# Dilated window attention with low-rank experts: batch rows as units, block-diagonal v, eight shared PSUM banks and an own list schedule

## The chip, the cores and the metric

The kernel runs on one core of one Trainium2 chip. The metric is device time in microseconds (us); lower is better. Kernel and changed kernel were each run twice for the main comparison. The kernel before took 156.75 us (median; 155.86 to 157.65). Each execution also leaves a span, from its first to its last instruction, which is 1.7 to 2.1 us shorter than its time in all runs of the record (1.8 in the profiled run of the changed kernel). A run counts as slow when it is over 1.5% above the fastest of its kernel.

Engine names in the profile: PE is the matmul engine (PEld its weight loads), DVE the vector engine, ACT the scalar engine, POOL the general engine that also issues the casting loads, SP the queue that issues stores. PSUM is the memory that matmuls write to; both kernels divide it into banks of 512 float32 columns, eight in all.

## The reference, cut to what matters

Eight batch rows, eight heads, 576 tokens, head dimension 64, float32. Heads 0 to 3 look back over 32 tokens, heads 4 to 7 over every fourth of 128. Then every token goes through two of eight rank-16 adapters.

```python
scores = scale * np.matmul(q, k.transpose(0, 1, 3, 2))
mask_plain = (rel >= 0) & (rel < 32)
mask_dil = (rel >= 0) & (rel < 128) & (rel % 4 == 0)
attn = softmax(np.where(mask, scores, -1e9))      # plain for heads 0-3, dilated for 4-7
x = np.matmul(attn, v)                            # then (B*S, H*D) = (4608, 512)
logits = x @ w_gate                               # 8 experts, the top two, weights by softmax
out = x + sum(w[e] * (x @ A[e]) @ B[e] for e in top2)
```

Names used below: the gates are `x @ w_gate` and all `x @ A` in one block of matmuls; the routing picks the top two experts; gz is `x @ A` times the chosen weights; the deltas are gz `@ B`, added to x at the end. aw holds A and w_gate, bt holds B.

Both kernels sort the tokens of the dilated heads by their remainder modulo 4, so that these heads become banded too. Keys come in blocks of 64 and each block is scored against the 96 queries that can see it. Inputs lie in memory as float32 and are cast to bf16 by the loads.

## The kernel before: the parts that matter here

All 4608 tokens are one stream, cut into nine units of 512 tokens; heads are taken in pairs (hp), one head on partitions 0 to 63, the other on 64 to 127. Per pair: a mask matmul for each of two banks, score matmuls on top, one exponential, value matmuls, normalisation by the sum column of v.

```python
ps_s = tile_pool(name="ps_s", bufs=2, space=PSUM)   # scores: 2 buffers of two banks
ps_o = tile_pool(name="ps_o", bufs=1, space=PSUM)   # values: one buffer of two banks
ps_m = tile_pool(name="ps_m", bufs=2, space=PSUM)   # transposes, gates, deltas
...
load(0); load(1)
nc.gpsimd.dma_start(out=AW, in_=aw)
nc.gpsimd.dma_start(out=BT, in_=bt)
nc.vector.tensor_scalar(BT, in0=BT, scalar1=0.5, scalar2=None, op0=ALU.mult)
...
def values(t, hp):                 # pairs of 64-row matmuls, one bank for each head of the pair
    ...
    for a in range(2):
        rows = slice(64 * a, 64 * a + 64)
        nc.tensor.matmul(op[:, a, 65 * u : 65 * u + 65],
                         lhsT=p[rows, at : at + 128], rhs=V[tv][rows, hp, blk], ...)
...
def after(t, hp):                  # gates and deltas of unit t-1, while unit t attends
    ...
steps = [(t, hp) for t in range(NU) for hp in range(4)]
for n, (t, hp) in enumerate(steps):
    scores(*steps[n + 1]); values(t, hp); after(t, hp)   # (cut)
```

The order on each engine is made from this program by a scheduler. Each unit's result is stored from a rotating buffer as soon as it is done.

The softmax here doesn't subtract the row's maximum and nothing guards it: scores larger than these inputs give would overflow.

Of the kernel before, what the change touches and what calls it, by code (L numbers as in the profile page):

```python
# [10 lines left out]
FP = mybir.dt.float32  # L11
# [5 lines left out]
NEG = -30000.0  # L17
B, H, S, D = 8, 8, 576, 64
W, C = 32, 4
E, R = 8, 16  # L20
NT = B * S
NU = NT // 512
ER = E * R
SEG = 96
PER = 192


def band(edges):


    k = np.arange(64)[:, None]
    w = np.arange(96)[None, :]
    ok = (w >= k) & (w - k < W)
    for e in edges:
        ok &= ~((k < e) & (w >= e))
    return np.where(ok, 0.0, NEG).astype(np.float32)


def masks():


    reg, cut = band(()), band((64,))
    mp = np.concatenate([reg, reg, cut, reg, reg, reg], 1)
    md = []
    for t in range(NU):
        edges = [144 * b for b in range(1, B)]
        first = band([e - 128 * t for e in edges])
        second = band([e - 128 * t - 64 for e in edges])
        before = band([e - 128 * t + 64 for e in edges])
        md += [first, second[:, 0:64], before[:, 64:96]]  # L50
    m = np.concatenate([mp] + md, 1)
    return np.concatenate([m, m], 0).astype(ml_dtypes.bfloat16)


NM = 6 * SEG + NU * 2 * SEG
# [3 lines left out]
def attn_adapters_kernel(  # L59
    ctx: ExitStack,  # L60
    tc: tile.TileContext,
    kq: bass.AP,
    vin: bass.AP,
    aw: bass.AP,
    bt: bass.AP,
    mk: bass.AP,
    idn: bass.AP,
    outp: bass.AP,
    outd: bass.AP,
):  # L70



# [4 lines left out]
    xpool = ctx.enter_context(tc.tile_pool(name="x", bufs=3))  # L78
    mpool = ctx.enter_context(tc.tile_pool(name="m", bufs=2))
    ps_s = ctx.enter_context(tc.tile_pool(name="ps_s", bufs=2, space=bass.MemoryType.PSUM))  # L80
    ps_o = ctx.enter_context(tc.tile_pool(name="ps_o", bufs=1, space=bass.MemoryType.PSUM))
    ps_m = ctx.enter_context(tc.tile_pool(name="ps_m", bufs=2, space=bass.MemoryType.PSUM))

    KQ = [one.tile([128, 4, 2, 512], BF, name=f"kq{t}") for t in range(NU)]
    V = [one.tile([128, 4, 8, D + 1], BF, name=f"v{t}") for t in range(NU)]
    ident = one.tile([128, 128], BF, name="ident")
    MK = one.tile([128, NM], BF, name="mk")
    AW = one.tile([128, 4, ER + E], BF, name="aw")
    BT = one.tile([ER, H * D], BF, name="bt")
    NP = 4  # L90
    P = [one.tile([128, 8 * PER], BF, name=f"p{i}") for i in range(NP)]

    nc.sync.dma_start(out=ident, in_=idn)
    nc.sync.dma_start(out=MK, in_=mk)
    for i in range(NP):
        nc.vector.memset(P[i].rearrange("p (s c) -> p s c", c=PER)[:, :, SEG:PER], 0.0)

    def load(t):
        if t == 0:
            for hp in range(4):  # L100
                nc.gpsimd.dma_start(out=KQ[t][:, hp], in_=kq[t, :, hp])
                nc.gpsimd.dma_start(out=V[t][:, hp], in_=vin[t, :, hp])
        else:
            nc.gpsimd.dma_start(out=KQ[t], in_=kq[t])
            nc.gpsimd.dma_start(out=V[t], in_=vin[t])

    load(0)
    load(1)
    nc.gpsimd.dma_start(out=AW, in_=aw)
    nc.gpsimd.dma_start(out=BT, in_=bt)  # L110
    nc.vector.tensor_scalar(BT, in0=BT, scalar1=0.5, scalar2=None, op0=ALU.mult)
    for t in range(2, NU):
        load(t)

    def prob(t, hp):
        return P[(4 * t + hp) % NP]

    def scores(t, hp):
        sp = ps_s.tile([128, 2, 512], FP, name="sps")
        for bk in range(2):  # L120
            if hp < 2:
                at = 0
                reg = True
                if t % 2 and t < 8 and (t - 1) // 4 == bk:
                    at = 2 if (t - 1) % 4 == 0 else 0
                    reg = False
                if reg:
                    mask = MK[:, 3 * SEG : 4 * SEG].unsqueeze(1).to_broadcast([128, 4, SEG])
                else:
                    mask = MK[:, at * SEG : (at + 4) * SEG].rearrange("p (s c) -> p s c", c=SEG)  # L130
            else:
                m0 = 6 * SEG + t * 2 * SEG
                mask = MK[:, m0 : m0 + 2 * SEG].unsqueeze(1).to_broadcast([128, 2, 2 * SEG])
            nc.tensor.matmul(  # L134
                sp[:, bk, 0 : 4 * SEG], lhsT=ident, rhs=mask, start=True, stop=False, skip_group_check=True
            )
        todo = []
        for s in range(8):
            if hp < 2 and s < 7 or hp >= 2 and s % 2 == 0:
                todo.append((s, 0, t, s, s, SEG))  # L140
            else:
                todo.append((s, 0, t, s, s, 64))
                if t:
                    todo.append((s, 64, t - 1, s, 0 if hp < 2 else s - 1, 32))
        for s, col, tk, kb, qb, n in todo:
            for a in range(2):
                rows = slice(64 * a, 64 * a + 64)
                at = SEG * (s % 4) + col
                nc.tensor.matmul(  # L149
                    sp[rows, s // 4, at : at + n],  # L150
                    lhsT=KQ[tk][rows, hp, 0, 64 * kb : 64 * kb + 64],
                    rhs=KQ[t][rows, hp, 1, 64 * qb : 64 * qb + n],
                    start=False, stop=True, skip_group_check=True,
                )
        nc.scalar.activation(  # L155
            prob(t, hp).rearrange("p (b s c) -> p b s c", b=2, c=PER)[:, :, :, 0:SEG],
            sp[:, :, 0 : 4 * SEG].rearrange("p b (s c) -> p b s c", c=SEG),
            AF.Exp, scale=scale,
        )

    X = {}

    def values(t, hp):
        st, hh = divmod(hp, 2)
        if hh == 0:
            X[t, st] = xpool.tile([128, 4, 4, D], FP, name=f"x{st}")
        x = X[t, st]
        p = prob(t, hp)
        op = ps_o.tile([128, 2, 512], FP, name="ops")
        for u in range(4):  # L170
            jobs = [(2 * u * PER, t, 2 * u), ((2 * u + 1) * PER - 64, t, 2 * u + 1)]
            if st == 0 and u:
                if (8 * t + 2 * u) % 9:
                    jobs.append(((2 * u - 1) * PER + 64, t, 2 * u - 1))
            elif st == 0:
                if t and (8 * t) % 9:
                    jobs.append((7 * PER + 64, t - 1, 7))
            elif t:
                jobs.append(((2 * u + 1) * PER + 64, t - 1, 2 * u + 1))
            for n, (at, tv, blk) in enumerate(jobs):  # L180
                for a in range(2):
                    rows = slice(64 * a, 64 * a + 64)
                    nc.tensor.matmul(  # L183
                        op[:, a, 65 * u : 65 * u + 65],
                        lhsT=p[rows, at : at + 128], rhs=V[tv][rows, hp, blk],
                        start=(n == 0), stop=(n == len(jobs) - 1), skip_group_check=True,
                    )
        o = op[:, :, 0 : 4 * 65].rearrange("p a (u d) -> p a u d", u=4)
        rec = mpool.tile([128, 2, 4], FP, name="rec")
        nc.vector.reciprocal(rec, o[:, :, :, D])  # L190
        nc.vector.tensor_tensor(  # L191
            x[:, :, 2 * hh : 2 * hh + 2].rearrange("p u a d -> p a u d"),
            o[:, :, :, 0:D], rec.unsqueeze(3).to_broadcast([128, 2, 4, D]), ALU.mult,
        )
        xb = mpool.tile([128, 4, 2 * D], BF, name=f"xb{hp}")
        nc.gpsimd.tensor_copy(xb, x[:, :, 2 * hh : 2 * hh + 2].rearrange("p u a d -> p u (a d)"))
        X[t, "b", hp] = xb

    M = {}

    def turn(t, st):
        tp = ps_m.tile([128, 1024], BF, name="mps")
        tv = tp.rearrange("p (k u i) -> p k u i", k=2, u=4)
        for hh in range(2):
            for u in range(4):
                nc.tensor.transpose(tv[:, hh, u], X[t, "b", 2 * st + hh][:, u], ident)  # L206
        xt = mpool.tile([128, 2, 512], BF, name=f"xt{st}")
        nc.scalar.copy(xt, tp.rearrange("p (k n) -> p k n", k=2))
        M[t, "xt", st] = xt

    def gates(t):
        xtp = M[t, "xt", 0].rearrange("p k (i c) -> p k i c", c=C)
        xtd = M[t, "xt", 1].rearrange("p k (c i) -> p k c i", c=C)
        zs = mpool.tile([128, C, ER + E], FP, name="zs")
        for half in range(2):
            zp = ps_m.tile([128, 2, ER + E], FP, name="mps")
            for cc in range(2):
# [151 lines left out]
```

## Time and profile before

| | kernel before |
|---|---|
| time, median of 2 | 156.75 us |
| span of the profiled run | 152.2 us |
| first score matmul, last value matmul | 8.0 us, 132.2 us |
| PE busy | 107.8 us, 71% of the span |
| loads done | about 81 us |
| one unit from 82 to 134 us | 10.4 us |

From the profile's page: the span, the busy time of each engine, then the span in 40 slices (tenths busy of PE, the granted PE clock in tenths, the busy share of the DMA engines).

```profile
span 152.2 us, 4604 instructions
PE 107.8 (71%) x2036; PEld 73.8 (49%) x2036; DVE 74.3 (49%) x194; ACT 61.1 (40%) x91; POOL 36.6 (24%) x66
PE   0279165989689627869967979989979887467150
PEclk9999955699689995555899999999999999975555
DMA  3999999999999999999970600602405106006015
```

PE has holes in the first half, exactly while DMA is full, and its clock falls there. The windows view gives busy time by stage (start and end, length, then PE, PEld, DVE, ACT and POOL busy with instruction counts, granted clock, DMA share, GB/s):

```profile
8.00:132.00 124.00, 98.76 (x1984) 68.58 (x1986) 63.66 (x170) 56.64 (x84) 31.05 (x53) 0.88 0.71 174
12.00:50.00 38.00, 28.53 (x656) 18.79 (x655) 11.10 (x26) 12.15 (x15) 9.99 (x19) 0.82 1.06 215
50.00:81.00 31.00, 22.13 (x302) 15.23 (x300) 15.97 (x44) 13.98 (x22) 7.18 (x13) 0.72 0.98 233
81.00:132.00 51.00, 44.90 (x976) 32.40 (x977) 36.50 (x100) 28.89 (x45) 11.75 (x18) 1.00 0.26 106
```

The Trainium skill, "TensorE: Matmul & The Clock Gate", Part 1, says that PE runs at half rate by default and that sustained activity releases it. The trace agrees: where PE has holes, between 12 and 81 us, the mean granted clock is 0.72 to 0.82, and it is 1.00 once the work is dense. A hole on PE is thus paid twice. The clock row is not to be trusted at the very start: it shows full clock before 15 us, yet the same two mask matmuls took longer there than later in the timeline (start, duration):

```profile
11.79 0.82 PE L134 MATMUL sps<-mk,ident 128*128 128x384 bf16 x2
29.79 0.50 PE L134 MATMUL sps<-mk,ident 128*128 128x384 bf16 x2
```

What one unit costs on PE at the full clock can be read from the chain of waits (start, duration, work):

```profile
29.33 0.53 PE sps L149 x24
29.86 0.43 PE sps L134 x2
30.29 0.48 PE ops L183 x24
30.77 0.46 PE sps L149 x18
92.37 0.61 PE mps L278 x4
95.11 0.55 PE mps L206 x8
97.18 0.95 PE mps L221 x14
111.95 0.40 PE mps L261 x4
```

Per pair: masks 0.43, scores 0.46 or 0.53, values 0.48; per unit besides: transposes 2 x 0.55, gates 16/14 of 0.95, gz transposes 0.40, deltas 2 x 0.61.

Two lines of the waits view (who waited for whom: total us, times, longest): its largest wait, and the one for bt:

```profile
DVE rec L190 <- PE ops L183: 28.9, 18, 9.4
DVE bt L111 <- DMA bt<-in_bt_dram: 8.6, 1, 8.6
```

### The profile page before, as it was taken

The page shows a single profiled execution, that of the slowest core. Times are in us where ns is not written, and L with a number is a line of the kernel's source. Part 1 is how long each engine was busy: PE and PEld are TensorE (multiplying, and loading weights), DVE is VectorE, ACT ScalarE, POOL GpSimd, SP SyncE. Part 2 cuts the span into 40 slices and gives each one's busy share as a digit, 9 for nine tenths or more (in the row PEclk, how much of TensorE's full clock was granted, in tenths as well). Part 3 has the DMA queues.
Part 4 walks back from the last instruction along what each step waited for, and adds up shares of the span by engine and source line. Part 5 has one row for each costly group of instructions (what it writes and reads, how often), then busy time and mean ns, then how long its engine had stood idle before and what let it go on. Part 6 is the DMA issues. An engine that isn't in the chain of part 4 may idle for free.

```text
span 152.2 us, 4604 instructions
## 1 busy us (share of the span) xinstructions
PE 107.8 (71%) x2036; PEld 73.8 (49%) x2036; DVE 74.3 (49%) x194; ACT 61.1 (40%) x91; POOL 36.6 (24%) x66
## 2 busy tenths in 40 slices
PE   0279165989689627869967979989979887467150
PEld 0045033656356514746655756756847656335020
DVE  3003103344240066175568578387677777770560
ACT  3023212345134640452463565583764653413110
POOL 7445014111116920111102122111341221310000
PEclk9999955699689995555899999999999999975555
DMA  3999999999999999999970600602405106006015
GB/s 101 179 203 221 210 211 216 223 205 220 211 221 214 216 207 224 232 274 269 216 276 14 273 6 22 261 4 118 161 0 236 48 0 249 33 18 258 3 57 219
DMA packets 6644, 24.86 MB, mean 163 GB/s; under 512 B 864, under 2 KB 1632, under 8 KB 5600
## 3 DMA queue, kind: packets, MB, share of 16 engines
q0 software_dynamic: 3744, 14.50, 47.9%
q1 hardware_dynamic: 2880, 10.06, 16.8%
q8 instruction: 16, 0.26, 0.7%
q14 instruction: 4, 0.03, 0.1%
HBM read 29.62 MB, written 9.44 MB: 257 GB/s over the span
## 4 chain that ended last, share of the span: by engine, by line
PE 46%; DVE 21%; DMA 14%; ACT 10%; issue 5%; POOL 1%; ACTq 0%; DVEq 0%; POOLq 0%
PE sps L149 10%; DMA bt<-in_bt_dram 9%; PE sps L134 8%; PE ops L183 8%; PE mps L278 7%; PE mps L221 6%; DMA kq_73<-in_kq_dram 5%; PE mps L206 4%; DVE gz L250 4%; PE mps L261 3%; ACT zs L225 2%; ACT gt L263 2%; ACT p_96 L155 2%; DVE eq L231 1%; DVE ms L233 1%
## 5 line engine op out<-in xcount | busy, mean ns | idle before, releaser
L134 PE MATMUL sps<-mk,ident 128*128 128x384 bf16 x72 | 22.9, 385 | 9.0 <-DMA mk<-in_mk_dram 5.6
L190 DVE RECIPROCAL rec<-ops 128x8 f32<-128x8 f32 x36 | 7.3, 204 | 29.1 <-PE ops L183 28.9
L278 PE MATMUL mps<-bt,gt 128*128 128x256 bf16 x72 | 15.4, 326 | 4.1 <-ACT gt L263 2.1
L155 ACT ACTIVATE p_95<-sps 128x768 bf16<-128x768 f32 x9 | 7.3, 812 | 18.4 <-PE sps L149 16.3
L155 ACT ACTIVATE p_97<-sps 128x768 bf16<-128x768 f32 x9 | 7.3, 810 | 10.2 <-PE sps L149 8.4
L278 PEld LDWEIGHTS <-gt 128*128 128x128 bf16 x72 | 7.1, 115 | 8.5 <-issue 3.5
L155 ACT ACTIVATE p_96<-sps 128x768 bf16<-128x768 f32 x9 | 7.3, 811 | 9.2 <-PE sps L149 7.0
L155 ACT ACTIVATE p_98<-sps 128x768 bf16<-128x768 f32 x9 | 7.3, 812 | 7.9 <-PE sps L149 4.9
L261 PE MATMUL mps<-ident,gz 128*128 128x128 bf16 x36 | 4.1, 247 | 8.5 <-DVE gz L250 8.5
L225 ACT COPY zs<-mps 128x272 f32<-128x272 f32 x18 | 6.7, 387 | 7.7 <-PE mps L221 7.4
L134 PEld LDWEIGHTS <-ident 128*128 128x128 bf16 x72 | 5.3, 101 | 9.3 <-issue 4.8
L263 ACT COPY gt<-mps 128x512 bf16<-128x512 bf16 x9 | 5.3, 585 | 10.1 <-PE mps L261 10.1
L183 PEld LDWEIGHTS <-p_98 64*128 64x128 bf16 x208 | 4.3, 100 | 6.3 <-DVE x_269 L191 2.0
L261 PEld LDWEIGHTS <-gz 128*128 128x128 bf16 x36 | 2.4, 107 | 9.8 <-DVE gz L250 9.7
L149 PEld LDWEIGHTS <-kq_74 64*64 64x64 bf16 x84 | 3.8, 134 | 6.7 <-DMA kq_74<-in_kq_dram 5.0
L183 PEld LDWEIGHTS <-p_96 64*128 64x128 bf16 x208 | 4.7, 103 | 4.7 <-issue 3.8
L149 PE MATMUL sps<-kq_74 64*64 64x96 bf16 (+1 forms) x64 | 3.4, 253 | 4.6 <-DMA kq_74<-in_kq_dram 4.6
L149 PEld LDWEIGHTS <-kq_73 64*64 64x64 bf16 x84 | 4.0, 153 | 4.5 <-DMA kq_73<-in_kq_dram 4.4
L183 PEld LDWEIGHTS <-p_97 64*128 64x128 bf16 x208 | 4.5, 103 | 3.4 <-DVE tt L239 1.7
L183 PEld LDWEIGHTS <-p_95 64*128 64x128 bf16 x208 | 4.6, 101 | 2.2 <-issue 1.3
L149 PE MATMUL sps<-kq_73 64*64 64x96 bf16 (+1 forms) x64 | 3.1, 268 | 2.4 <-DMA kq_73<-in_kq_dram 2.4
L149 PEld LDWEIGHTS <-kq_75 64*64 64x64 bf16 x84 | 3.2, 108 | 2.6 <-issue 2.4
(359 smaller groups left out, 279.3 us busy)
## 6 DMA issues: line engine op xcount, KB each, us to landing
kq_73<-in_kq_dram POOLq DMA_DIRECT2D x4, 256.0 KB, 8.3
kq_74<-in_kq_dram POOLq DMA_DIRECT2D x1, 1024.0 KB, 12.3
kq_75<-in_kq_dram POOLq DMA_DIRECT2D x1, 1024.0 KB, 16.8
kq_76<-in_kq_dram POOLq DMA_DIRECT2D x1, 1024.0 KB, 22.3
kq_77<-in_kq_dram POOLq DMA_DIRECT2D x1, 1024.0 KB, 23.3
kq_78<-in_kq_dram POOLq DMA_DIRECT2D x1, 1024.0 KB, 27.5
kq_79<-in_kq_dram POOLq DMA_DIRECT2D x1, 1024.0 KB, 29.3
kq_80<-in_kq_dram POOLq DMA_DIRECT2D x1, 1024.0 KB, 30.1
```

The costliest lines, as they stand in the source:

```text
L134: nc.tensor.matmul(sp[:, bk, 0 : 4 * SEG], lhsT=ident, rhs=mask, start=True, stop=False, skip_group_check=True)
L149: nc.tensor.matmul(sp[rows, s // 4, at : at + n], lhsT=KQ[tk][rows, hp, 0, 64 * kb : 64 * kb + 64], rhs=KQ[t][rows, hp, 1, 64 * qb : 64 * ...
L155: nc.scalar.activation(prob(t, hp).rearrange("p (b s c) -> p b s c", b=2, c=PER)[:, :, :, 0:SEG], sp[:, :, 0 : 4 * SEG].rearrange("p b (s ...
L183: nc.tensor.matmul(op[:, a, 65 * u : 65 * u + 65], lhsT=p[rows, at : at + 128], rhs=V[tv][rows, hp, blk], start=(n == 0), stop=(n == len(j ...
L190: nc.vector.reciprocal(rec, o[:, :, :, D])
L206: nc.tensor.transpose(tv[:, hh, u], X[t, "b", 2 * st + hh][:, u], ident)
L221: nc.tensor.matmul(zp[:, cc], lhsT=xt, rhs=AW[:, kk], start=(kk == 0), stop=(kk == 3), skip_group_check=True,)
L225: nc.scalar.copy(zs[:, 2 * half : 2 * half + 2], zp)
L250: nc.vector.tensor_tensor(gz.rearrange("p c (e r) -> p c e r", e=E), zs[:, :, 0:ER].rearrange("p c (e r) -> p c e r", e=E), g2.unsqueeze(3 ...
L261: nc.tensor.transpose(tp[:, 128 * c : 128 * (c + 1)], M[t, "gz"][:, c], ident)
L263: nc.scalar.copy(gt.rearrange("p (i c) -> p i c", c=C), tp.rearrange("p (c i) -> p i c", c=C))
L278: nc.tensor.matmul(dp[:, a], lhsT=lhs, rhs=BT[:, 256 * st : 256 * st + 256], start=True, stop=True, skip_group_check=True,)
```

## The change

Its intent is to keep every engine filled. A unit becomes one whole batch row (576 tokens), so no band crosses a unit's edge. v is stored block-diagonally, the two heads of a pair on different partitions and columns with zeros between, so one 128-row matmul of 130 columns serves both heads and its result fits one bank. Rows live in a ring of four slots. PSUM becomes eight single banks that everybody shares. The output stays resident, and its stores wait for the last loads. The order on every engine comes from a list schedule in the kernel, with a duration for each operation.

```diff
-NT = B * S
-NU = NT // 512
+NB = 9
+NS = 4
+NP = 4
+class Op:  # name, engine, duration (ns), what it waits for, priority, banks it takes and frees
+class Plan:
+    def order(self):     # simulates the engines; the earliest start, then priority, wins
+        ...
+    BS = [psum.tile([128, 512], FP, name=f"bs{i}") for i in range(8)]
+    plan = Plan({"s": 8, "p": NP, "xb": 4, "xt": 2, "zs": 2, "gz": 2, "g": 2})
...
-        sp = ps_s.tile([128, 2, 512], FP, name="sps")
+            banks = [buf(("S", b, hp), BS, k) for k in range(2)]
+            for k in range(2):
+                rows = slice(64 * k, 64 * k + 64)        # masks: 64 rows each, side by side
...
-                for a in range(2):
-                    rows = slice(64 * a, 64 * a + 64)
-                    nc.tensor.matmul(
-                        op[:, a, 65 * u : 65 * u + 65],
-                        lhsT=p[rows, at : at + 128], rhs=V[tv][rows, hp, blk],
+                    nc.tensor.matmul(
+                        o[:, 130 * r : 130 * r + 130].rearrange("p (a d) -> p a d", a=2),
+                        lhsT=p[:, at : at + 128], rhs=bdv(b, hp, j),
...
+            nc.gpsimd.tensor_copy(                       # a new reorder of the gated tokens, on POOL
+                buf(("g", b), GN).rearrange("p (i c) -> p c i", c=C),
+                buf(("g", b), GD).rearrange("p (c i) -> p c i", c=C),
+            )
...
+    gate = f"L{B - 1}01"                                 # stores wait for the last row's first load
+        add(f"S{b}{hp}", "PE", 620, ...)                 # scores of a pair: planned 620 ns
+        add(f"V{b}{st}{k}", "PE", (440, 440, 530)[k], ...)
+        add(f"K{b}", "PE", 300, ...)                     # gz transposes
+        add(f"M{b}", "POOL", 680, ...)                   # the reorder
+    with tc.manual_schedule():
+        for op in plan.order():
+            op.emit()
```

gz moves from DVE to POOL, and the adapters' weights are loaded first on the SP queue and cast on ACT.

## The prediction

> **What bounds the kernel now.** Three stages, from the windows view. (a) 0 to about 25 us: little runs. PE waits 5.0 us for the second unit's keys, and DVE sits 8.6 us (waits view) in front of the scaling of bt, whose load queues behind 1.5 units of loads; the normalisations are behind it. DMA is saturated: 212 GB/s of bf16 written, so 424 GB/s of fp32 read. The Trainium skill, "DMA: Bandwidth & Descriptors", Specifications, gives 435 GB/s as the fabric ceiling; the trace agrees. (b) 25 to 134 us: PE-bound with gaps. From 82 to 134 us one unit of 512 tokens takes 10.4 us (start to start of the gate transposes in the chain of waits); PE is busy 44.6 of 52 us, DVE 38.0, ACT 28.7, DMA a quarter. Earlier the granted clock falls to 0.55 in places. (c) 134 to 152 us: the last unit's chain, PE clock 0.53.
>
> **What changes.** Eight units of 576 tokens instead of nine of 512 with seams.
> - PE: 2036 matmuls become about 1500. Values 832 -> 416: 130 columns on 128 rows instead of pairs of 65 columns on 64 rows; instructions fall, columns streamed don't. Masks: two 64-row matmuls (480, 384 columns) side by side instead of two of 384 in sequence. Per batch I estimate: scores with masks 2.6 us (18 score matmuls took 0.46 in the trace), values 52 x 57 ns = 2.9, transposes 1.1, gates 20 x 65 ns = 1.3, deltas 1.1: about 9.1 us.
> - DVE: normalisation in six pieces of 384 columns. From the trace (512 columns 692 ns, 8 columns 204 ns) a piece is about 560 + 200 ns; routing about 1.5 us, five additions 3.2 us: 9.3 us a batch. gz (0.69 us) moves to POOL, where it is slower.
> - ACT: exponentials 572 + 492 ns four times, transposed copies 2.9 us, the rest 1.8: 8.9 us a batch.
> - POOL: casts (0.61 us for 512 columns), gz, one reorder, load issues: about 7 us.
> - DMA: the same bytes in; 28.5 MB at 424 GB/s is 8.4 us a batch, ending near 72 us instead of 80. Stores (9.44 MB at about 390 GB/s, 24 us) wait until the last loads, then drain under compute.
>
> So all are balanced near 9 us a batch, and the gain is overlap: eight shared banks and ordering by list remove the waits for the single "ops" buffer and for whole stages, and bt no longer blocks DVE.
>
> **Sum.** First normalisation at about 11 us; eight batches at 9.3 us with about 93% filling = 80 us; the last batch's chain after its attention (cast, transpose, gates, routing, gz, transpose, delta, store), serial, about 11 us net of what is counted: span about 103 us. Unprofiled time is 4.5 us above the span before: **108 us, range 99 to 120**. Chances: faster by over 2% 0.97, within 2% 0.01, slower 0.02.
>
> **What would show it.** Loads ended by 70 to 76 us; no DVE wait over 3 us after the start; between 20 and 80 us PE, DVE and ACT each over 80% busy and a period of 9.5 to 10.5 us a batch; granted clock near 1 there; stores landing after 72 us, off the chain except the last; a serial tail of 12 to 18 us.
>
> **What would make it wrong.** A fixed order jams where real durations differ from the planned (POOL waiting for old loads in front of casts, gz above 1.5 us on POOL): period 11 to 12 us and 120 us or more. Half-width loads (64 partitions) running at less than full rate: loads bind at over 10 us a batch. Clock throttling under denser PE work.

## The result, and the profile after

The changed kernel took 121.39 us (median; 120.8 and 121.98). The ratio, that is the mean time of its fast runs over that of the kernel before in the same rounds (so not quite the ratio of the two medians), is 0.774, with a 95% interval of 0.760 to 0.788. The direction was right. The time lies 13.4 us above the stated 108 and outside the range of 99 to 120.

The page's lines of after:

```profile
span 119.0 us, 3669 instructions
PE 92.2 (77%) x1496; PEld 69.2 (58%) x1496; DVE 75.2 (63%) x220; ACT 70.4 (59%) x155; POOL 59.4 (50%) x86
PE   0105979999999999999999989999999915910540
PEclk9999999999999999999999999999999997695555
DMA  3999999999999999999999999998640053009054
```

The windows view of after:

```profile
9.00:95.00 86.00, 82.81 (x1429) 63.49 (x1430) 58.74 (x172) 59.94 (x137) 48.66 (x69) 1.00 0.93 227
95.00:119.00 24.00, 8.84 (x68) 5.56 (x67) 9.73 (x30) 4.48 (x11) 6.16 (x5) 0.67 0.36 147
20.00:91.00 71.00, 69.81 (x1234) 53.36 (x1233) 51.65 (x156) 50.32 (x117) 41.24 (x58) 1.00 0.96 241
```

From 20 to 91 us PE is busy 69.8 of 71 us at the full clock. In the waits view PE waits only 1.0 us in all from 20 to 95 us (four waits). DVE, whose 9.3 us a batch the prediction took for the period, is busy 51.7 of 71 us, ACT 50.3; so its sign "PE, DVE and ACT each over 80% busy" failed for both (73% and 71%). (The Trainium skill's front page, "Trainium Kernel Development and Optimization", Performance Expectations, warns that matmul busy time is a bad measure of closeness to the roofline, since matmuls are pipelined. It still named the right engine here, but only e1 below proves that.)

Where the 33 us of span went, divided at the start of the first score matmul and at the end of the last value matmul:

| stage | before | after |
|---|---|---|
| start to first score | 8.0 us | 9.4 us |
| first score to last value | 124.2 us | 85.9 us |
| last value to the end | 20.0 us | 23.7 us |

All of the gain is in the middle; the tail became longer, and the start differs by no more than it varies from run to run (see the experiments). What one row costs on PE now, from the chain of waits of after:

```profile
38.38 0.47 PE bs L329 x8
43.56 0.46 PE bs L462 x5
45.27 0.44 PE bs L486 x4
47.37 0.54 PE bs L486 x4
47.91 0.23 PE bs L498 x4
48.14 1.41 PE bs L403 x20
49.55 0.33 PE bs L371 x4
51.39 0.27 PE bs L290
51.66 0.52 PE bs L298 x18
52.18 0.39 PE bs L371 x5
61.52 0.81 PE bs L329 x14
62.33 0.24 PE bs L340 x4
```

Masks and scores 4 x 0.80 (0.27 and 0.53), values 2 x (0.47 + 0.81 + 0.24), transposes 2 x (0.33 + 0.39), gates 1.41, gz transposes 0.46, deltas 0.44 + 0.54 + 0.23: 10.8 us per 576 tokens. The gate blocks of successive rows start at 25.28, 36.64, 48.14, 59.37, 71.50, 82.77 and 91.80 us, 11.1 us apart on average (the first five intervals 11.5, the last 9.0). So the change took no work off PE (10.6 before, 10.8 after, for the same tokens): values became dearer, 3.0 us against 2.2, and masks with scores cheaper, 3.2 against 4.2. What it did was to fill PE and, with that, to hold its clock: 98.8 of 124 us busy at 0.88 became 82.8 of 86 us at 1.00. Of the 38 us, some 16 are thus shorter busy time, and 22 are idle time filled.

The tail, from the timeline of after (start, duration, engine, line, operation, and in brackets the idle time before it):

```profile
100.59 2.58 PE L403 MATMUL bs<-aw,xt 128*128 128x136 bf16 x20
103.70 2.48 DVE L508 TENSOR_TENSOR x<-x,bs 128x512 f32<-128x512 f32 x4 [5.87 <-PE bs L486]
106.43 0.19 DVE L424 TENSOR_REDUCE sm<-zs 128x5 f32<-128x40 f32 x1
108.54 1.27 POOL L449 TENSOR_TENSOR gz<-zs,sm 128x640 bf16<-128x640 f32 x1 [5.60 <-DVE sm L444]
111.45 1.46 POOL L472 COPY gn<-gd 128x576 bf16<-128x576 bf16 x1 [1.64 <-ACT gd L467]
114.82 0.41 DVE L515 TENSOR_TENSOR x<-x,bs 128x256 f32<-128x256 f32 x1
```

The last gates take 2.58 us instead of 1.4, because PE has gone cold. Their copies are done at 103.66 us, but the last routing starts at 106.43, since DVE first does row 6's additions. Then come gz, the reorder and the last additions, one after another.

### The profile page after: what moved, and what is told of

Its sections match the earlier page's. It is cut to its first block, busy times and chain, and to the rows that moved or that the text cites. A ratio compares the mean times of both kernels' runs of the same rounds, so it can differ in the third digit from the quotient of the medians.

```text
span 119.0 us, 3669 instructions
## 1 busy us (share of the span) xinstructions
PE 92.2 (77%) x1496; PEld 69.2 (58%) x1496; DVE 75.2 (63%) x220; ACT 70.4 (59%) x155; POOL 59.4 (50%) x86
## 4 chain that ended last, share of the span: by engine, by line
PE 60%; DMA 13%; DVE 8%; POOL 8%; issue 5%; POOLq 1%; ACT 1%; DVEq 0%; ACTq 0%
PE bs L329 14%; DMA slot<-in_kv_dram 13%; PE bs L298 12%; PE bs L403 10%; PE bs L371 6%; PE bs L290 6%; PE bs L486 5%; DVE x L508 3%; POOL slot L232 3%; PE bs L462 2%; PE bs L340 2%; POOL gz L449 2%; DVE x L352 1%; POOLq L636 1%; POOL gn L472 1%
## 5 line engine op out<-in xcount | busy, mean ns | idle before, releaser
L363 POOL CAST xb<-x 128x512 bf16<-128x512 f32 (+1 forms) x32 | 21.3, 671 | 30.7 <-DVE sm L444 15.3
L309 ACT ACTIVATE p<-bs 128x480 bf16<-128x480 f32 x64 | 30.9, 538 | 9.0 <-PE bs L298 7.8
L329 PE MATMUL bs<-slot,p 128*128 128x130 bf16 x352 | 27.4, 224 | 1.0 <-ACT p L309 1.0
L352 DVE TENSOR_TENSOR x<-bs,rc 128x384 f32<-128x384 f32 x48 | 26.8, 557 | 1.6
L508 DVE TENSOR_TENSOR x<-x,bs 128x512 f32<-128x512 f32 x32 | 20.2, 682 | 11.6 <-PE bs L486 11.4
L329 PEld LDWEIGHTS <-p 128*128 128x128 bf16 x352 | 21.8, 98 | 2.7 <-ACT p L309 1.7
L298 PE MATMUL bs<-slot 64*64 64x96 bf16 (+1 forms) x576 | 18.8, 208 | 5.6 <-DMA slot<-in_kq_dram 5.4
L298 PEld LDWEIGHTS <-slot 64*64 64x64 bf16 x576 | 14.7, 109 | 13.3 <-issue 6.8
L232 POOL DMA_DIRECT2D slot<-in_kv_dram x32 | 16.7, 532 | 7.3 <-DMA slot<-in_kq_dram 4.7
L472 POOL COPY gn<-gd 128x576 bf16<-128x576 bf16 x8 | 11.8, 1475 | 4.8 <-ACT gd L467 4.8
L391 ACT COPY xt<-bs 128x512 bf16<-128x512 bf16 x16 | 9.4, 587 | 6.5 <-PE bs L371 6.2
L381 ACT COPY xt<-bs 128x512 bf16<-128x512 bf16 x16 | 9.4, 591 | 4.2 <-PE bs L371 4.1
L403 PEld LDWEIGHTS <-xt 128*128 128x128 bf16 (+1 forms) x160 | 10.7, 106 | 1.5 <-issue 0.2
```

The costliest lines, as they stand in the source:

```text
L232: insts[name] = nc.gpsimd.dma_start(out=dst, in_=src)
L298: nc.tensor.matmul(banks[k][rows, SEG * c : SEG * c + n], lhsT=t[rows, 0, 64 * j : 64 * j + 64], rhs=t[rows, 1, 64 * j : 64 * j + n], star ...
L309: nc.scalar.activation(buf(("P", b, hp), P)[:, 5 * k : 5 * k + n, 0:SEG], buf(("S", b, hp), BS, k)[:, 0 : n * SEG].rearrange("p (j c) -> p ...
L329: nc.tensor.matmul(o[:, 130 * r : 130 * r + 130].rearrange("p (a d) -> p a d", a=2), lhsT=p[:, at : at + 128], rhs=bdv(b, hp, j), start=(n ...
L352: nc.vector.tensor_tensor(X[b][:, st, 3 * k : 3 * k + 3].rearrange("p r (a d) -> p r a d", a=2), o[:, :, :, 0:D], rc.unsqueeze(3).to_broad ...
L363: nc.gpsimd.tensor_copy(buf(("xb", b, hp), XB)[:, 0:n], X[b][:, st, 4 * h : 4 * h + n])
```

## The experiments

Eighteen runs were made after the result, in five groups (two of them repeat a kernel); one group shares a chip and its runs of the kernel before, whose median was 153.4 to 155.1 us in them. Times are medians of all executions of a kernel (four with 3 rounds, six with 5), slow ones included; what is compared are the fast ones, and a table at the end of this section has their means and ratios. Starts vary: in the profiled runs of these kernels the first score came at 7.4 to 9.8 us, with the first load, so I also compare stages. The theory after the result was A: PE's work binds from 20 to 91 us and was under-counted. Rivals: B, DVE or the fixed order binds; C, the loads bind until 72 us.

### What sets the period: e1, e3, e4

e1 leaves out the mask matmuls (wrong result):

```diff
-                nc.tensor.matmul(banks[k][:, 0 : n * SEG], lhsT=two[rows], rhs=mask, start=True, stop=False, ...)
...
-                        start=False, stop=True, skip_group_check=True,
+                        start=True, stop=True, skip_group_check=True,
```

> The 64 mask matmuls are left out (wrong result on purpose; the last score matmul streams 96 columns so that nothing uninitialised is read). Theory A, PE is the bound from 20 to 91 us: the masks take 0.27 us of each 0.80 us score block, 4 per batch, so about 1.08 us per batch less on PE, period 11.4 -> 10.3 us, total 113 to 115 us instead of 121.4. Rival B (DVE or POOL, or the fixed order, binds, and PE only fills): under 2 us faster, PE shows new idle time in 30 to 90 us. Rival C (loads bind): no change before 72 us.

e3 computes reciprocals for the first row only (wrong):

```diff
-            nc.vector.reciprocal(rc, o[:, :, :, D])
+            if b == 0:
+                nc.vector.reciprocal(rc, o[:, :, :, D])
```

> Reciprocals are computed in the first batch only (wrong result on purpose): 42 of 48 are gone, 0.19 us each, about 1.15 us per batch off DVE. Theory A (PE binds): under 1.5 us faster, and that from the tail. Rival B1, the prediction's (DVE binds at 9.3 us per batch): about 7 us faster.

e4 loads a quarter of the columns for rows 4 to 7 (wrong):

```diff
+                n = V1 // 4 if b >= NS else V1
-   ... sl[0:64, st, 0:V1], kv[b, st, 0:64] ...
+   ... sl[0:64, st, 0:n], kv[b, st, 0:64, 0:n] ...
```

> Loads of batches 4 to 7 fetch a quarter of the columns, the rest is what the slot held (wrong result on purpose). Theory A: within 1 us of 121.4, loads done near 50 us, the same period of 11.4 us per batch. Rival C (loads bind until 72 us and PE waits for data or for POOL queued behind loads): 4 us or more faster.

Measured: e1 114.24 us, e3 120.2 us, e4 121.57 us. The fast runs of the unaltered changed kernel average 121.4 us, and 120.7 us in the control a0 below (another chip). Removing 1.08 us per row, 8.6 in all, from PE brought 6 to 7 us (fast runs 114.6); by stage, some 5 us of it lie between first score and last value (81.2 us against 85.9, and 86.9 in a0). Removing 1.15 us per row from DVE brought 1.5 to 2.2 us, within the scatter (fast runs 119.2 us; the stage 85.1 us), where rival B asked for 7. Removing more than a third of the load bytes brought nothing; rows 0 to 3 still loaded in full there. Theory A stands; B (as far as DVE goes) and C (for the later rows) fall. What the order is worth is tried below. Not all of the 8.6 us came back, and in e1 PE is less full than before, 94% instead of 98%, but still by far the fullest engine:

```profile
20.00:84.00 64.00, 60.16 (x1138) 49.49 (x1136) 49.81 (x151) 48.77 (x115) 39.64 (x56) 1.00 1.03 253
```

(The windows view of e1: 60.2 of 64 us busy on PE.)

### What block-diagonal v is for: e2, e6, e9

e2 goes back to pairs of 64-row value matmuls in the new schedule. The two row halves write two neighbouring banks, so each piece of values takes two banks instead of one. The zero fills fall away.

```diff
-                        o[:, 130 * r : 130 * r + 130].rearrange("p (a d) -> p a d", a=2),
-                        lhsT=p[:, at : at + 128], rhs=bdv(b, hp, j),
+                    for a in range(2):
+                        nc.tensor.matmul(
+                        o[:, a, 65 * r : 65 * r + 65],
+                        lhsT=p[64 * a : 64 * a + 64, at : at + 128], rhs=vrows(b, hp, j, a),
...
-                    alloc=[("s", ("O", b, st, k), 1)], ...
+                    alloc=[("s", ("O", b, st, k), 2)], ...        # two neighbouring banks
```

> Undoes the block-diagonal v alone: values again as pairs of 65-column matmuls on 64 rows each, into two neighbouring banks, in the same list schedule; no zero filling of the slots. If row pairs run side by side, as in the kernel before (24 of them in 0.48 us against 8 block-diagonal ones in 0.47 us and 22 in 1.27 us here), a batch's values take about 2.2 us instead of 3.0: theory A 115 to 118 us. If fewer instructions are what matters (the change's presumable intent), it is slower than 121.4: 123 to 128 us, from twice the instructions or from two banks for each piece.

It took 124.95 us: my theory missed, it was slower. Yet the values themselves are shorter on PE (in its chain of waits 16 of the half matmuls take 0.36 us, against 0.47 us for 8 whole ones), and PE is busy only 63.8 of 71 us between 20 and 91 us. e6 is e2 with the planner's durations set to measured ones (next section):

> Row-tiled values (as in e2_rowtiled) with measured durations in the planner. In e2 PE was busy only 16.8 of the 20 us from 40 to 60 us and waited behind deltas for the reorder on POOL. If that loss came from the order, the shorter values now show: 115 to 118 us. If it comes from the two banks for each piece of values, it stays near 124 us.

It took 123.18 us (on a chip where e5, the block-diagonal kernel with the same durations, took 115.82), so the order made for wrong durations was not the cause. The rest of the suspicion was the banks. e9 is the block-diagonal kernel with measured durations (e5), in which each piece reserves two neighbouring banks and uses one:

```diff
-                    alloc=[("s", ("O", b, st, k), 1)], ...
+                    alloc=[("s", ("O", b, st, k), 2)], ...        # the second stays unused
```

> The replanned kernel with block-diagonal values (e5, 115.8 us) in which each piece of values reserves two neighbouring PSUM banks and uses one. If the row-tiled kernels lost because of the two banks that they need (shared-bank theory): 120 to 124 us, near e6's 123.2. If they lost because of the row-tiled matmuls themselves (mode switches, twice the instructions): stays at 115 to 117 us.

It took 126.28 us, against 115.82 and 117.32 us for the same kernel with one bank in two other groups (ratios to the kernel before 0.823, and 0.755 and 0.762). The windows view of e5, then that of e9:

```profile
20.00:91.00 71.00, 70.67 (x1249) 55.26 (x1244) 52.95 (x158) 52.39 (x122) 42.51 (x58) 1.00 0.96 240
```

```profile
20.00:91.00 71.00, 66.01 (x1095) 50.27 (x1094) 48.02 (x140) 45.88 (x106) 38.11 (x53) 1.00 0.93 227
```

In the same 71 us, PE does 1095 matmuls instead of 1249. In the waits view of this stretch PE waits 4.7 us, 4.5 of them for normalisations on DVE, which free the banks; in e5 it waits 0.2 us. So the gain of block-diagonal v is neither fewer instructions nor shorter values: it is that a piece of output occupies one bank of eight. At two banks each, the row pairs are even the faster ones (e6 0.797, e9 0.823). Whether the cost comes from two banks as such or from their having to be neighbours was not separated. Why two banks were needed for row pairs: the Trainium skill, "TensorEngine Tiling (Array Packing)", Restrictions and Gotchas, says that different row tiles (here the two halves of 64 rows) write to different PSUM banks. No run here tried two row halves on the same partitions of one bank. (The profiled run of e9 was a slow one; the verdict rests on its six timed runs, all above 125 us.)

### The planned durations: e5, e13, e12, e15

e5 changes only the numbers that the planner is given:

```diff
-            add(f"S{b}{hp}", "PE", 620, ...
+            add(f"S{b}{hp}", "PE", 800, ...
-        add(f"K{b}", "PE", 300, ...
+        add(f"K{b}", "PE", 460, ...
-        add(f"M{b}", "POOL", 680, ...
+        add(f"M{b}", "POOL", 1490, ...
 (values 480, 480, 610 for 440, 440, 530; transposes 330, 390 for 240, 300; gates 850, 570 for 780, 500; deltas 260 for 220; five more by 6% or less, or up to 14% shorter)
```

> Only the planner's durations are changed, to what the trace shows (score block 800 ns for 620, the reorder on POOL 1490 for 680, gates 850 and 570 for 780 and 500, gz transposes 460 for 300, and so on), so the order changes and nothing else. If the gap between the 10.8 us of PE work and the 11.4 us period, and part of the tail, comes from an order made for wrong durations: 118 to 120 us. If the order hardly matters because PE is full anyway: within 1 us of 121.4.

115.82 us, and 115.75 to 118.89 us (median 117.32) when taken again as e15:

> The kernel of e5_replan once more with five rounds: 115 to 117 us, and a ratio to the kernel before of 0.745 to 0.765; b3 with its changed tail is then within 1 us of it.

The order was worth 4 to 6 us, more than expected. By stages, first score to last value went from 85.9 us (86.9 in the control a0 below) to 84.2 in e5 (84.5 in e15), and the tail from 23.7 (23.9) to 20.9 (21.7): some 4.5 us in all. Between 20 and 91 us PE was 98% busy already and is 99.5% busy in e5, so little was left there; about half of the gain is in the tail. Why the tail is shorter was not tested.

The largest wrong duration is the reorder on POOL: 680 planned, 1475 ns measured. e13 keeps the changed kernel's order and turns the reorder's loops, so that it writes runs and reads with a stride:

```diff
-                buf(("g", b), GN).rearrange("p (i c) -> p c i", c=C),
-                buf(("g", b), GD).rearrange("p (c i) -> p c i", c=C),
+                buf(("g", b), GN).rearrange("p (i c) -> p i c", c=C),
+                buf(("g", b), GD).rearrange("p (c i) -> p i c", c=C),
```

> The changed kernel, same order of instructions; only the reorder on POOL walks its output instead of its input, so that it writes runs and reads with a stride. If the strided writes are what made it slow: 0.65 to 0.8 us each instead of 1.47, and, if deltas behind it were what held PE back, 118 to 120 us instead of 121.4 to 122. If the cost is in the element count: no change in either.

The group of the reorder in the view of groups (count, busy us and mean ns, idle before), in the changed kernel and in e13:

```profile
L472 POOL COPY gn<-gd 128x576 bf16<-128x576 bf16 x8 | 11.8, 1475 | 4.8 <-ACT gd L467 4.8
```

```profile
L472 POOL COPY gn<-gd 128x576 bf16<-128x576 bf16 x8 | 9.3, 1168 | 4.7 <-ACT gd L467 4.7
```

Under half of the hoped-for drop, and no change of the time: 121.64 us. Five of its six runs counted as slow, so its verdict stays unclear, but its six runs (119.25 to 122.72) lie where the control's lie, and so do its stages (87.3 and 23.6 us, in a slow run). e12 does the same swap with measured durations in the planner:

> The same swap with measured durations in the planner (750 for the reorder). If the 6 us of e5 came from the other durations (score blocks, gates, transposes): 114 to 115.5 us. If they came from the reorder, e13 alone reaches 116 and this is no faster than it.

117.76 us, the same as e5 within the scatter; again five of six runs counted as slow and the verdict is unclear. As far as these two runs go, the gain of e5 came from the order, and neither from the cost of the reorder nor from its planned duration. Which of the dozen durations matters most was not separated.

### The tail: e7a, e7b, b2, b3

e7a fills PE's gaps after the last values with 45 matmuls of 512 columns whose result nobody reads:

```diff
+    for i in range(45):
+        add(f"F{i}", "PE", 230, [...], 1000, filler(), ...)   # lhsT=ident, rhs=CB[:, 0:512]
```

> 45 matmuls of 512 columns that nobody reads fill PE's gaps after the last values, so that its clock stays up: the last gates should take 1.4 us instead of 2.5, deltas and transposes of the last batch about 1 us less in all: 1.5 to 2.5 us faster than 121.4. If the clock does not follow or the fillers delay the real work: 0 or slower.

118.69 us. The clock follows; in its timeline the last gates take

```profile
100.99 1.48 PE L403 MATMUL bs<-aw,xt 128*128 128x136 bf16 x20
```

and the tail is 22.6 us instead of 23.7. The gain is seen in the trace and is small, because the rest of the tail does not run on PE; in the times it is hardly clear of the noise (ratio 0.761 to 0.783, the control 0.782 to 0.796).

e7b puts gz and the reorder of the last row on DVE, and row 7's last normalisation and routing ahead of waiting additions:

```diff
+            (nc.vector if b == B - 1 else nc.gpsimd).tensor_tensor(       # gz; the reorder likewise
-        ... f"D{b}{st}{half}"], t + 5.2 + n / 2, total(b, st, half)
+        ... f"D{b}{st}{half}"], t + 5.2 + n / 2 + {5: 10, 6: 6.4}.get(b, 0), total(b, st, half)
```

> In the last batch gz and the reorder run on DVE instead of POOL, and DVE does the last normalisation and the last routing ahead of the additions of batches 5 and 6, for which they waited (routing about 2.7 us, normalisation 1.7 us). Theory: the tail is DVE order plus a slow POOL: 3 to 5 us faster. If the last chain is held by other things (PE clock, stores): under 1.5 us.

119.07 us (116.33 to 120.36), verdict unclear because three of its four runs counted as slow; in its profiled run, one of those, the tail is 20.9 us, and the reorder took 0.80 us on DVE instead of 1.47 on POOL. b2 joins replanning, warm PE and such a tail (the reorder on ACT for the last two rows); b3 adds the swapped reorder.

> Measured durations in the planner, PE kept warm by unread matmuls after the last values, the reorder on ACT for the last two batches, gz on DVE for the last, and batch 6's routing and what follows it behind the last attention. If the stream (period) and the tail add independently: 115.8 minus 2 to 5: 110 to 114 us. If replanning already took what e7a and e7b showed: 114 to 116.

> As b2 with the swapped reorder: the reorder on ACT takes 0.65 us instead of 1.47 in the last two batches, off the last chain: 114 to 116 us, 1 us below b2. The rest of the tail (last values to the end, 20 us in b2) is a chain of latencies of some 17 instructions and stays.

b2 took 116.85 us and b3 116.70 us. Their tails are 20.1 and 19.3 us, the latter from a run that counted as slow; but first score to last value took 85.6 and 87.4 us, longer than the 84.2 and 84.5 of e5 and e15. They do not differ from e5 and e15 (115.82 and 117.32 us) by more than the groups do from each other. So some 4 of the 24 us of tail could be taken away, 2 to 3 of them by the order of e5 alone; at least 19 us were left in every kernel that I tried. The reorder did not become cheap on ACT: it took 1.47 us there in b2 and 1.17 us in b3, the same as on POOL, and 0.65 was expected.

### The control and the stores: a0, e10

The changed kernel again, as a control, and the changed kernel with its stores issued as soon as their sums are done:

> The changed kernel once more, unaltered, as a control beside the next three: 120 to 122.5 us, same period of 11.4 us between gate blocks.

```diff
-        add(name + "_i", "SP", 450, deps + [gate], prio, ...
+        add(name + "_i", "SP", 450, deps, prio, ...
-            if b < B - 1:
-                tc.add_manual_dep(i.ins, insts[gate].ins.name, SYNC, reason="after the loads")
```

> Stores of batches 0 to 6 are issued when their sums are done, not behind the last loads. PE theory: loads have slack after the first two batches (e4 showed no gain from fewer), so the stores slow them but not the kernel: within 1.5 us of 121.4. If holding stores back was worth something: 2 us or more slower, with PE waiting for loads.

121.97 us for the control, 123.96 us with early stores (ratios to the kernel before 0.789, 0.782 to 0.796, and 0.804, 0.798 to 0.810: the intervals just part). Holding the stores back is worth about 2 us (fast runs 122.9 against 120.7), the second branch of the expectation, if only just. Its first score to last value is 88.8 us against 86.9. That branch also named PE waiting for loads as the cause, and this is not shown: from 20 to 91 us PE is busy 70.0 us in both.

### The start of the kernel before: e8, e14

e8 is the kernel before with aw and bt loaded first on the SP queue and cast on ACT, so DVE no longer waits for bt:

```diff
-    nc.gpsimd.dma_start(out=BT, in_=bt)
-    nc.vector.tensor_scalar(BT, in0=BT, scalar1=0.5, scalar2=None, op0=ALU.mult)
+    nc.sync.dma_start(out=BTF, in_=bt)
+    nc.scalar.mul(BT, BTF, 0.5)            # aw likewise
```

> The kernel before, with aw and bt loaded first on the SP queue and cast on ACT; nothing else. If DVE's 8.6 us wait for bt was a main loss of the kernel before: 5 to 9 us faster. If units were held by their own loads and by the order of stages anyway: under 3 us.

155.28 us, ratio 1.005 (0.994 to 1.016): nothing. The 8.6 us wait that the prediction named for the start cost no time that these runs can see. The first gates still stood at 52.5 us (51.1 before), because on PE they come after 288 value matmuls, three units' worth. e14 gives the kernel before two x buffers instead of three, which moves them behind 194:

```diff
-    xpool = ctx.enter_context(tc.tile_pool(name="x", bufs=3))
+    xpool = ctx.enter_context(tc.tile_pool(name="x", bufs=2))
```

> The kernel before with two x buffers instead of three: the scheduler then puts unit 0's first transposes behind 194 value matmuls instead of 288, one unit earlier (about 9 us). If attention running ahead of the gates, which leaves more than five units of gates for after the loads, is what cost the kernel before: 3 to 8 us faster. If it stays at 154 or is slower, the early part is held by the loads or by two buffers.

154.6 us, ratio 1.010 (1.002 to 1.018): no gain either, and perhaps a loss of 1%. The first gates moved only to 49.8 us. Between 12 and 50 us PE was busy 22.6 of 38 us instead of 28.5, and from 50 to 81 us 25.6 of 31 instead of 22.1: what was won late was lost early. So what held the old stream is settled only negatively: not the wait for bt, and not one unit of run-ahead. Nor does the waits view of the kernel before name one wait: of the 18.3 us that PE waits from 12 to 81 us, 4.6 are for the second unit's keys, 3.3 for gz in two waits, and the rest is in eleven entries of at most 1.9 us. A kernel before with smaller loads, which would have tried the loads as the cause, was not run.

### All runs side by side

Where only one run was fast, there is no ratio. Where two kernels are compared above, it is by these intervals.

| run | median of all, us | mean of fast runs, us (number) | ratio to the kernel before, 95% |
|---|---|---|---|
| changed kernel | 121.39 | 121.4 (2) | 0.760 to 0.788 |
| a0 control | 121.97 | 120.7 (3) | 0.782 to 0.796 |
| e1 no masks (wrong) | 114.24 | 114.6 (4) | 0.738 to 0.761 |
| e3 few reciprocals (wrong) | 120.20 | 119.2 (2) | 0.764 to 0.795 |
| e4 fewer loads (wrong) | 121.57 | 121.3 (4) | 0.782 to 0.804 |
| e2 row pairs | 124.95 | 123.9 (2) | 0.805 to 0.833 |
| e6 row pairs, replanned | 123.18 | 122.1 (2) | 0.786 to 0.807 |
| e9 two banks, replanned | 126.28 | 125.8 (4) | 0.817 to 0.828 |
| e5, e15 replanned | 115.82, 117.32 | 115.8 (4), 116.8 (4) | 0.746 to 0.764, 0.752 to 0.771 |
| e13 reorder turned | 121.64 | 119.3 (1) | none |
| e12 the same, replanned | 117.76 | 115.6 (1) | none |
| e7a warm PE | 118.69 | 118.4 (3) | 0.761 to 0.783 |
| e7b tail on DVE | 119.07 | 116.3 (1) | none |
| b2, b3 | 116.85, 116.70 | 115.8 (3), 115.6 (3) | 0.758 to 0.768, 0.748 to 0.763 |
| e10 early stores | 123.96 | 122.9 (3) | 0.798 to 0.810 |
| e8 before, bt early | 155.28 | 153.8 (3) | 0.994 to 1.016 |
| e14 before, two x buffers | 154.60 | 154.5 (6) | 1.002 to 1.018 |

## Why the prediction was wrong, point by point

Right: the direction; that the loads would end near 72 us and not bind (the page's GB/s rise there from 215 to over 350, when the stores take over, and e4 shows slack); that the gain is overlap and not less work; that the clock would hold; that stores would drain under compute.

Wrong, by the terms of its sum (span about 103 us, plus 4.5):

| term | predicted | measured | miss |
|---|---|---|---|
| first normalisation | 11 us | 12.1 us | +1.1 |
| from there to the end of the last normalisation | 80 us | 85.6 us | +5.6 |
| the rest | 11 to 12 us | 21.3 us | about +9.5 |
| time above the span | 4.5 us | 1.8 us | -2.7 |
| sum | 108 us | 121.4 us (the terms give 120.8, the profiled run) | +13 |

1. The step that failed first is "Per batch I estimate: scores with masks 2.6 us ..., values 52 x 57 ns = 2.9, transposes 1.1, gates 20 x 65 ns = 1.3, deltas 1.1: about 9.1 us". It measured 10.8. Scores with masks are 3.2 (the masks take 0.27 before the scores can start, and 18 score matmuls 0.53), transposes 1.44, gates 1.41, deltas 1.21, values 3.04; the gz transposes, 0.46, were left out. Hence "eight batches at 9.3 us with about 93% filling = 80 us" rested on the wrong engine: with its filling that is 10.0 us a row, below the 10.8 us of PE work, and 10.7 were measured (85.6 us for eight). DVE's 9.3 us was right (75.2 us busy in all, about 9.4 a row with the start's fills), but it does not bind: e1 and e3 show it. Doing the same sum for the kernel before would have warned me: it gives 9.4 us per 512 tokens, or 10.6 us for 576.

2. The tail, "serial, about 11 us net of what is counted", is the larger miss. Its own list left out the reorder (1.47 us); the store and the end took 3.8 us after the last addition. Summed from the timeline without waits and at full clock the chain after the last normalisation is, by my estimate, about 16.5 us. The remaining 5 us are, as read from the timeline, the cold clock (the last gates 1.1 us longer), DVE doing row 6's additions before the last routing (2.8 us) and PE's order (0.7 us). The statement "a serial tail of 12 to 18 us" failed too: 23.7 us after the last value matmul. That e7a, b2 and b3 shortened it by 1 to 4 us fits this split but does not show its parts: e5, which changed nothing but the order, took off 2.8 us. A period of "9.5 to 10.5 us a batch" failed as well: 11.1.

3. "Unprofiled time is 4.5 us above the span" compared the profiled run of one execution with the median of others. The difference of one execution is 1.7 to 2.1 us in all runs (1.8 in the profiled run of the changed kernel); the kernel before simply varies by some 5 us between executions. This error hid part of the other two.

4. "A fixed order jams where real durations differ from the planned" was named as a risk, with 120 us or more for it. It came true in part: planned durations were short on PE by about 20% for scores and 35% for gz transposes, and by half for the reorder, and e5 shows that right ones are worth 4 to 6 us. The period was 11.1 us as that sentence has it, but for reason 1.

5. "bt no longer blocks DVE" was counted among the causes of the gain. e8 shows that it is worth nothing by itself.

What carries the gain of 33 us of span is shown only in part: one bank for each piece of values (9 to 10 us between e5 or e15 and e9) and stores behind the loads (2 us). That the rest comes from the shared banks and the list order is argued from the filling of PE (98.8 of 124 us at 0.88 against 82.8 of 86 us at 1.00), not shown by a run. It also stays open what kept PE idle in the kernel before while the loads ran. And the size of the gain is best read from the control: there the ratio is 0.789 from more runs, because the kernel before took 153.4 us in that group and 156.75 in the main comparison.

The best versions measured are e5 (115.8 and, again, 117.3 us), b2 (116.85 us) and b3 (116.7 us), which cannot be told apart; all are correct and faster than the changed kernel (121.4 and 122.0 us).

## What to carry to other kernels

Before predicting a rescheduled kernel, add up each engine's work per token in the old trace and in the new plan with durations measured in their context, switches and small blocks included: if the two sums agree, the gain can only come from filling (and, with it, from the clock), and the largest sum is the floor. A long wait in a profile is a cause only if something that ends last stands behind it; change that one wait and see. When PSUM is shared, count the banks that a piece of output holds before counting the matmuls that make it.

## What the Trainium skill lacked or had wrong

- "TensorE: Matmul & The Clock Gate", Part 1, the note on HAM trace caveats (HAM is the block that gates PE's clock), says that clock events in traces can be unreliable, and that the clock has been seen stuck low for over 50 us. The profiled execution of e12 looks like a case: it took 164.5 us, its gate blocks took 2.5 us instead of 1.4, and yet the view of cores has the full clock throughout (its page has no clock row at all). The lines are PE's busy time from the page and the core's clock from the view of cores, then two of its gate blocks in the chain of waits. (It counts as a slow run.) What the page lacks is that such a state can hold for one whole execution, of a kernel whose other five took 115.6 to 118.2 us, and leave no clock event; that PE ran slowly is inferred from the durations.

```profile
PE 143.5 (88%) x1496; PEld 101.5 (62%) x1496; DVE 76.9 (47%) x220; ACT 71.3 (44%) x155; POOL 57.9 (36%) x86
```

```profile
core 0: 162.7 us, clock 1.000
```

```profile
28.84 2.52 PE bs L403 x20
45.54 2.51 PE bs L403 x20
```

- "TensorEngine Tiling (Array Packing)", Gotcha 1, says that different row tiles cannot access the same PSUM bank simultaneously. Both kernels write one bank from two row halves with 64x64 tiles, on different partitions, and are correct; 18 such matmuls, of 96 columns but for the last two, take 0.53 us, 29 ns each. One alone should take 43 ns, an estimate from this trace's 8 value matmuls of 130 columns in 0.47 us; so the two halves overlap. The sentence should tell the same partitions from different ones, as the page "PSUM — Partial Sum Buffer" does when it counts such a collision by bank and 32-partition quadrant.
- "GPSIMD Engine Reference", Performance pitfalls for Q7 kernels, gives a cost for reads whose step is over 8 bytes, in custom kernels. For a plain copy on POOL the trace shows the other side: 576 bf16 elements written with a step of 8 bytes took 1475 ns, read with a step of 288 bytes and written in runs 1168 ns. ACT took the same times for the same two copies (1472 and 1166 ns), while its copy of as many elements out of PSUM takes 653 ns. I found no page with such times for a plain copy, on POOL or on ACT; "SBUF — State Buffer" has only a general rule on strides over 16-byte lines, without a time.
